# Decay attention with a low-rank mixer and feed-forward: ScalarE's casts of the next q and k set behind the newest exponential

## The chip, the cores and the metric

The kernel runs on 1 core of one Trainium2 chip, in one launch. The metric is device time in microseconds (us) of that core. Before the change it is 1206.89 us, the median of 3 runs (1206.88 to 1207.52).

## The reference

Eight batches of eight heads, 576 positions, 64 numbers per head. Attention with a learned decay comes first, then a block over the joined heads that mixes positions at low rank and applies a feed-forward layer. Cut to what is computed:

```python
scores = (q @ k.T) / 8                         # per batch and head, 576 x 576
cum    = cumsum(log(clip(f, 1e-4, 1)))
scores = where(causal, -1e9, scores + cum[:, None] - cum[None, :])
attn   = exp(scores - max(scores)); attn = attn / (sum(attn) + 1e-9)
x      = attn @ v                              # joined to 8 x 576 x 512
u      = x + ((x.T @ U @ V).T)                 # rank 32 over the positions
out    = u + relu(u @ w_ch1) @ w_ch2           # 512 -> 2048 -> 512
```

Everything is float32. The kernel gets that precision from a faster matmul format (fp32r) by splitting each operand into a high half, which is a cast, and a low half, which is the operand less its cast, and by adding two or three products.

## The kernel before, in words

**Two stages.** The first stage (to about 680 us) runs attention for all batches and the feed-forward for six of its sixteen column chunks, batch by batch. The second (from there to the end) runs the other ten chunks. The change is in the first.

**Steps and slots.** Heads are taken two at a time: 32 pairs, numbered 0 to 31. `step(t)` works on three pairs at once: scores of pair p, the turning of the probabilities of pair p-1 (called a) and their product with v, and the low-rank product of pair p-2 (called c). It has ten slots, s = 0 to 9. A slot first runs what earlier slots deferred to it (`run_later`, in order of a phase number), then issues its own TensorE work, and last some mixing or feed-forward units of an earlier batch. After every fourth pair come the mixing units of a whole batch; these steps are called mixing steps below.

**Names.** In the rows below the pair's number is left out. `S_10` is the score of half 1 (the second head) and row block 0; `St` are the two tails; `nm` the negated row maximum; `P_10` the exponential of `S_10`; `T_10` the transposed probabilities of half 1, group 0; `PTh` and `PTl` their high and low halves; `Tt` the low-rank product (U against x); `V` the product with v, and `cr` the copy of its lower rows. `G` are two operand tiles that hold the split q and k: G[0] for the first head (the first half) and G[1] for the second.

**One slot's chain.** For the score of one row block: TensorE forms it in one of two PSUM banks of the pool `psS` (lines 365 and 366), VectorE adds the mask and takes the row maximum (line 386), and ScalarE takes the exponential (line 394). The next score but one needs the bank, so TensorE waits for that exponential. Likewise a transposed group (line 461) lies in one of two banks of `psT`: ScalarE copies the high half (line 440), VectorE subtracts for the low half (line 443), and then the bank is free. In slot 8 the order on TensorE is S_12, T_12, Tt: Tt (line 630) takes the bank that T_11 of slot 7 had.

**The split of the next pair.** `parts(p, j, engines)` makes G[j] for pair p: two casts on ScalarE (line 328, q and k, 128 x 576 each), and on GpSimd a cast (line 328 again) and two subtractions (lines 343 and 344). The first half of pair p+1 is called in slot 6 of step p, after the last use of G[0]; the second half in slot 0 of the pair's own step.

**Who sets the order.** TensorE and SyncE (which issues the DMAs) run in the order in which the code is written. ScalarE, VectorE and GpSimd are ordered when the kernel is built, by a list scheduler that takes the written order, the dependencies and its own estimate of when each operand is there. `behind(ins, kind)` adds an edge without a semaphore: `ins` is ordered after the newest instruction of that kind. In the kernel before, the casts of the first half are set behind the exponential of the tails (line 422, kind "tail"), and those of the second half are free. For pair 6, the first one that is split, `pin` keeps the written order.

Of the kernel before, what the change touches and what calls it, by code (L numbers as in the profile page):

```python
# [36 lines left out]
NF = 6  # L37
# [3 lines left out]
def tile_decay_attention_moe(ctx, tc, qk, v, f, U, V, w1, w2, out):  # L41
    nc = tc.nc
# [8 lines left out]
    newest = {}  # L51

    def behind(ins, kind):
        tc.add_manual_dep(
            ins.ins, newest[kind].ins.name,
            mybir.DependencyInfo(mybir.DependencyClass.NoSync, mybir.DependencyReason.DATA), reason=f"order behind {kind}",
        )
# [104 lines left out]
    def decay_split(fr, dq, cm):  # L162
        nc.vector.tensor_scalar(cm[:, 2], fr, -8.0, None, op0=ALU.mult)
        nc.gpsimd.tensor_tensor(cm[:, 3], dq[:, 1], cm.bitcast(F32)[:, 2], op=ALU.subtract)
# [101 lines left out]
    def defer(phase, fn, slots=1):  # L266
        later.setdefault(now[0] + slots, []).append((phase, fn))

    def run_later():
        now[0] += 1  # L270
        for _, fn in sorted(later.pop(now[0], []), key=lambda x: x[0]):
            fn()
# [54 lines left out]
    def copy(eng, dst, src):  # L327
        return eng.copy(dst, src) if eng is nc.scalar else eng.tensor_copy(dst, src)  # L328

    def parts(p, j, engines):  # L330


        g, cols, own, oth = G[j], COLS[j], OWN[j], OTH[j]
        q, k = st[p]["qk"][j]
        gf = g.bitcast(F32)
        eq, ek, ek2, el, em = engines
        pin = tc.keep_in_program_order if p == NF else lambda x: x
        for eng, dst, src in ((eq, g[:, 0, cols], q), (ek, g[:, 2, cols], k)):
            cast = pin(copy(eng, dst, src))
            if j == 0 and p > NF:  # L340
                behind(cast, "tail")
        pin(copy(ek2, g[own, 3, cols], k[own]))
        pin(el.tensor_tensor(g[oth, 2, cols], k[oth], gf[oth, 2, cols], op=ALU.subtract))  # L343
        pin(em.tensor_tensor(g[own, 1, cols], q[own], gf[own, 0, cols], op=ALU.subtract))  # L344
# [13 lines left out]
    def qk_mm(ps, p, c0, cols, first, last, j):  # L358

        if p < NF:  # L360
            q, k = st[p]["qk"][j]
            nc.tensor.matmul(ps, q[:, c0 : c0 + P], k[:, cols], start=first, stop=last)  # L362
            return
        cols = slice(AOFF[j] + cols.start, AOFF[j] + cols.stop)
        nc.tensor.matmul(ps, G[j][:, 0, c0 : c0 + P], G[j][:, 2, cols], start=first, stop=False)  # L365
        nc.tensor.matmul(ps, G[j][:, 1, c0 : c0 + P], G[j][:, 3, cols], start=False, stop=last)  # L366
# [3 lines left out]
    def bank_s(p, name):  # L370

        scored[0] += 1
        if p < NF and scored[0] % 2:
            return psF.tile([P, 512], F32, tag="F", name=name)
        return psS.tile([P, 512], F32, tag="S", name=name)

    def score(p, j, i):
        z = st[p]
        w = P * (i + 1)
        ps = bank_s(p, f"S{p}_{j}{i}")  # L380
        c0 = AMAIN[j] + P * i
        qk_mm(ps[:, :w], p, c0, slice(0, w), True, True, j)
        col = 2 * i + j

        def top():
            newest["top"] = nc.vector.tensor_tensor_reduce(  # L386
                ps[:, :w], ps[:, :w], mask[:, 512 - w : 512], scale=-SCALE, scalar=3.0e38,
                op0=ALU.add, op1=ALU.min, accum_out=z["nm"][:, col : col + 1],
            )

        def use():
            pt = sb2.tile([P, w], F32, tag=f"P{i}", name=f"P{p}_{j}{i}")
            z["P"][j].append(pt)
            nc.scalar.activation(  # L394
                pt, ps[:, :w], AF.Exp, bias=z["nm"][:, col : col + 1], scale=-1.0, accum_out=z["sm"][:, col : col + 1]
            )

        defer(0, top)
        defer(2, use)
# [372 lines left out]
    NP = B * NHP  # L772
# [49 lines left out]
    def step(t):  # L822
        p = SEQ[t]
# [3 lines left out]
        nxt_p = p + 1 if ps_ else NP  # L827
# [6 lines left out]
        for s in range(6 + 2 if last else SLOTS):  # L834
            when = now[0] + 1

            def at(phase, fn):
                later.setdefault(when, []).append((phase, fn))

            if s == 0 and ps_ and p >= NF:  # L840
                at(5, lambda: parts(p, 1, ENGINES))
                place_decay(p, 1)
            if (t, s) == (1, 1):
                decay_split(fr, dq, cm0)
            if (t, s) == (2, 1):
                for j in range(2):
                    decay_negate(cm0, j)
                nc.vector.tensor_scalar(fl, cm0.bitcast(F32)[:, 2], 0.0, 1.0, op0=ALU.mult, op1=ALU.add)
            if (t, s) == (3, 2):
                decay_store(cm0, fl)  # L850
            if (t, s) == (NHP, 0):
                clear_operands()
            if s == 3 and pa and a >= NF:
                at(4, lambda: make_vs(a))
            if s == (9 if pa and a >= NF else 4) and pa:
                at(4, lambda: inverse(a))
            if s == 6 and NF <= nxt_p < NP:
                at(5, lambda: parts(p + 1, 0, ENGINES))
            if s == (4 if last else 5) and px:
                at(5, lambda: split_x(c))  # L860
            if (t, s) in DECODES:
                u = DECODES.index((t, s))

                steps = [lambda: load_w(u + (3 if u < 6 else 2)), lambda: decode_w(u)]
                if u < LATE:
                    for fn in steps if u < 8 else steps[::-1]:
                        at(6, fn)
                else:
                    at(6, lambda: decode_w(u, (0,)))
                    defer(6, lambda: decode_w(u, (1,)), 3)  # L870
                    defer(6, steps[0], 3)
            run_later()
            if s == 4 and ps_ and p > NF:
                load_v(p)
            if s == 1 and pa and 0 < a <= NF:
                load_v(a)
            if s == 0 and ps_ and p:
                load_qk(p + 1, 0)
            if s == 6 and ps_ and p:
                load_qk(p + 1, 1)  # L880
            if s == 7 and NF <= nxt_p < NP:
                place_decay(p + 1, 0)

            if ps_:
                if s < 4:
                    score(p, 0, s)
                elif s < 6:
                    score_tail(p, s - 4)
                elif s > 6:
                    score(p, 1, s - 6)  # L890
            if px and s == 0:
                values(c, 1)
            if pa and s < 3:
                turn_p(a, 0, s)
            if px and s == (2 if last else 3):
                turn_x(c)
            if s == (3 if last else 4) and (pa or px):
                turn_small(a if pa else None, c if px else None)
            if pa and s == 5:
                turn_tail(a)  # L900
            if pa and 6 <= s < 9:
                turn_p(a, 1, s - 6)
            if pa and s == 7:
                values(a, 0)
            if px and s == (6 if last else 8):
                ranks(c)

            if mixing:
                for _ in range(2 if t == MIX[0] and s < 3 else 1):
                    mixing.pop(0)[1]()  # L910
                for _ in range(1 if ending else (1, 1, 2, 1, 1)[s] if s < 5 else 0):
                    if filler:
                        run_filler()
            elif len(filler) > held(t) and s in ROOM:

                ahead = sum(x >= s for x in ROOM) + len(ROOM) * (min(m for m in MIX if m > t) - 1 - t)
                credit[0] += (len(filler) - held(t)) / max(ahead, 1)
                if credit[0] > 0.999 or t > LAST - 3:
                    credit[0] = max(credit[0] - 1, 0)
                    run_filler()  # L920
            if ps_ and s == 6:
                score(p, 1, 0)
            if last and s == 7:
                run_filler()
            if px and s == (6 + 1 if last else 9) and st[c]["hp"] == NHP - 1:
                b = st[c]["b"]
                assert len(filler) <= held(t) and not mixing
                mixing.extend(mix_units(b))
                nxt = ffn_units(b)
                pending.append(nxt)  # L930
            if not mixing and pending:
                assert not filler
                filler.extend(pending.pop())
# [715 lines left out]
```

## Time and profile before

| | before |
|---|---|
| median of 3 runs | 1206.89 us |
| time of the profiled execution | 1206.92 us |
| its span, first to last instruction | 1205.1 us |
| TensorE (PE) busy | 1183.8 us, 98% |
| VectorE (DVE) busy | 931.2 us, 77% |
| ScalarE (ACT) busy | 767.3 us, 64% |
| GpSimd (POOL) busy | 514.8 us, 43% |
| ScalarE casts into G (line 328) | 104, 65.4 us busy, 684 ns each |

The profiled execution takes 1.8 us more than its span and is within 0.03 us of the median. A row of the timeline gives the start in us, the duration in us, the engine, the line, the operation, what it writes and reads, the shape and how many were merged into the row; square brackets give the time for which the engine stood idle before it and what ended that. PEld is TensorE's loading of weights. A row of the waits gives who waited, for whom, the sum in us, how often, and the longest.

### The profile page before, as it was taken

Reading aid. Unit: us, or ns where it says so; the run is one execution under the profiler, and the core shown is the slowest. Engines: PE = TensorE matmul, PEld = TensorE weight load, DVE = VectorE, ACT = ScalarE, POOL = GpSimd, SP = SyncE. Lnnn points to the kernel's source line nnn. Section 1 sums busy time; section 2 is a strip of 40 time slices with the busy share of each in tenths; the row PEclk is TensorE's granted clock in tenths of the full one; section 3 lists DMA queues with packets and bytes.
Section 4 is the critical chain, followed back from the end, with each engine's and each line's share of the span. In section 5 each row is a group of like instructions: output and inputs, shape, how many; then the busy total and the mean of one; then the engine's idle time right before and its main releaser. Section 6 shows DMA issues by size and latency. Waiting matters only on the chain.

```text
span 1205.1 us, 23859 instructions
## 1 busy us (share of the span) xinstructions
PE 1183.8 (98%) x8460; PEld 1084.9 (90%) x8460; DVE 931.2 (77%) x2233; ACT 767.3 (64%) x2076; POOL 514.8 (43%) x506
## 2 busy tenths in 40 slices
PE   8999999999999999999999999999999999999998
PEld 5888898998998988989989997788999999999998
DVE  8987878778778678877686699976777867778675
ACT  8877786776868758767766577434454544545543
POOL 2215463553635435544442000024575555555553
PEclk9999999999999999999999999999999999999999
DMA  5754244335335325425322244533424344243420
GB/s 161 192 139 146 81 104 155 103 82 160 84 89 169 102 69 152 121 69 172 90 79 90 97 144 160 159 105 94 134 86 110 101 133 134 96 115 99 132 52 36
DMA packets 81159, 138.47 MB, mean 115 GB/s; under 512 B 8752, under 2 KB 45616, under 8 KB 78992
## 3 DMA queue, kind: packets, MB, share of 16 engines
q1 hardware_dynamic: 79824, 128.56, 35.4%
q0 software_dynamic: 1152, 8.39, 3.8%
q8 instruction: 67, 1.10, 0.4%
q14 instruction: 52, 0.43, 0.1%
q10 hardware_dynamic: 64, 0.00, 0.0%
HBM read 101.08 MB, written 35.78 MB: 114 GB/s over the span
## 4 chain that ended last, share of the span: by engine, by line
PE 83%; DVE 8%; ACT 6%; issue 1%; POOL 0%; ACTq 0%; DVEq 0%; POOLq 0%
PE N L1283 12%; PE A L723 12%; PE B L742 11%; PE A L1263 9%; PE B L1263 7%; PE V L564 5%; PE T L461 4%; PE S L365 3%; PE V L536 3%; PE S L366 2%; PE B L1283 2%; PE Tt L630 2%; PE S L362 2%; PE O L1348 1%; ACT G L328 1%
## 5 line engine op out<-in xcount | busy, mean ns | idle before, releaser
L394 ACT ACTIVATE P<-S,nm 128x128 f32<-128x128 f32 (+3 forms) x256 | 139.0, 545 | 54.5 <-DVE nm L386 48.8
L197 POOL TENSOR_TENSOR hb<-xn,hb 128x256 fp32r<-128x256 f32 x136 | 113.6, 856 | 125.5 <-ACT hb L194 108.0
L386 DVE CUSTOM_DVE_ANT_0 S<-S,mask 128x128 f32<-128x128 f32 (+3 forms) x256 | 125.8, 496 | 52.3 <-PE S L366 46.3
L328 POOL CAST G<-qk 64x576 fp32r<-64x576 f32 x52 | 35.4, 680 | 206.9 <-PE St L366 150.4
L723 PE MATMUL A<-uh,w1h 128*128 128x256 f32 (+1 forms) x384 | 119.7, 312 | 0.0
L723 PE MATMUL A<-ul,w1h 128*128 128x256 f32 (+1 forms) x384 | 113.6, 296 | 0.0
L723 PE MATMUL A<-uh,w1l 128*128 128x256 f32 (+1 forms) x384 | 113.5, 296 | 0.0
L194 ACT CAST hb<-xn 128x256 fp32r<-128x256 f32 x136 | 51.8, 404 | 77.3 <-DVE xn L1269 42.8
L443 DVE TENSOR_TENSOR PTl<-T,PTh 128x512 fp32r<-128x512 f32 (+1 forms) x156 | 79.0, 527 | 12.1 <-ACT PTh L440 11.1
L742 PE MATMUL B<-w2h,hh 128*128 128x512 f32 x216 | 88.2, 408 | 0.0
L461 PE MATMUL T<-ident,P 128*128 128x128 f32 x544 | 85.5, 273 | 0.0
L344 POOL TENSOR_TENSOR G<-qk,G 64x576 fp32r<-64x576 f32 x52 | 74.6, 1434 | 24.6 <-ACT G L328 24.3
L742 PE MATMUL B<-w2l,hh 128*128 128x512 f32 x216 | 85.0, 394 | 0.0
L742 PE MATMUL B<-w2h,hl 128*128 128x512 f32 x216 | 84.6, 392 | 0.0
L1283 PE MATMUL N<-sw,hb 128*128 128x256 f32 x546 | 80.4, 283 | 0.0
L1283 PE MATMUL N<-b2h,hb 128*128 128x256 f32 x420 | 79.9, 282 | 0.0
L343 POOL TENSOR_TENSOR G<-qk,G 64x576 fp32r<-64x576 f32 x52 | 75.0, 1442 | 10.9 <-issue 4.2
L365 PE MATMUL S<-G 128*128 128x128 f32 x208 | 70.8, 345 | 7.0 <-ACT P L394 5.8
L723 PEld LDWEIGHTS A<-uh,w1h 128*128 128x128 f32 x384 | 72.9, 190 | 0.9 <-DVE hl L728 0.2
L723 PEld LDWEIGHTS A<-uh,w1l 128*128 128x128 f32 x384 | 73.1, 190 | 0.5
L723 PEld LDWEIGHTS A<-ul,w1h 128*128 128x128 f32 x384 | 72.8, 190 | 0.0
L1283 PEld LDWEIGHTS N<-sw,hb 128*128 128x128 f32 x546 | 71.7, 190 | 0.4 <-POOL hb L197 0.2
(328 smaller groups left out, 4006.3 us busy)
## 6 DMA issues: line engine op xcount, KB each, us to landing
qk<-in_qk_dram SPq DMA_DIRECT2D x104, 288.0 KB
direct<-ud SPq DMA_DIRECT2D x48, 256.0 KB
sr<-in_w_dram SPq DMA_DIRECT2D x20, 512.0 KB
vr<-in_v_dram SPq DMA_DIRECT2D x32, 256.0 KB
accd<-ost SPq DMA_DIRECT2D x32, 256.0 KB
xn<-accd SPq DMA_DIRECT2D x8, 1024.0 KB
out_dram<-xn SPq DMA_DIRECT2D x32, 256.0 KB
ud<-uh SPq DMA_DIRECT2D x7, 1024.0 KB
```

The lines of the kernel that those rows point to most:

```text
L197: leng.tensor_tensor(dl, src, dh.bitcast(F32), op=ALU.subtract)
L343: pin(el.tensor_tensor(g[oth, 2, cols], k[oth], gf[oth, 2, cols], op=ALU.subtract))
L344: pin(em.tensor_tensor(g[own, 1, cols], q[own], gf[own, 0, cols], op=ALU.subtract))
L365: nc.tensor.matmul(ps, G[j][:, 0, c0 : c0 + P], G[j][:, 2, cols], start=first, stop=False)
L386: newest["top"] = nc.vector.tensor_tensor_reduce(ps[:, :w], ps[:, :w], mask[:, 512 - w : 512], scale=-SCALE, scalar=3.0e38, op0=ALU.add, o ...
L394: nc.scalar.activation(pt, ps[:, :w], AF.Exp, bias=z["nm"][:, col : col + 1], scale=-1.0, accum_out=z["sm"][:, col : col + 1])
L443: defer(2, lambda: nc.vector.tensor_tensor(dstl, src, dsth.bitcast(F32), op=ALU.subtract))
L461: nc.tensor.transpose(tp[:, P * x : P * x + P], z["P"][j][i][:, P * c : P * c + P], ident)
L723: nc.tensor.matmul(ps[:, :nt], wt[:, fc, c], ut[:, c, sl], start=m == 0, stop=m == 3 * NDC - 1)
L742: nc.tensor.matmul(ps, ht[:, fc, P * x : P * x + P], wt[:, fc], start=fc == 0 and m == 0, stop=fc == NA - 1 and m == 2,)
L1263: nc.tensor.matmul(ps, a[x][:, c], b[y][:, c], start=start and m == 0, stop=m == 5, skip_group_check=not start)
L1283: nc.tensor.matmul(ps[:, y], a[p_][:, P * y : P * y + P], w[q_], start=start and y == 0 and m == 0, stop=stop and y == 1 and m == 2,)
```

## The change

Two edits in `parts`, `score` and `step`:

- every exponential of a row block is noted as the newest of kind "exp", and for all pairs after 6 the ScalarE casts of both halves are set behind the newest one. In the first half this takes the place of the edge to the tail's exponential; in the second half there was none;
- the first half of the next pair is called in slot 7 instead of 6 (for pair 6 itself it stays in slot 6). GpSimd's cast and subtractions are called with it.

```diff
@@ parts @@
         for eng, dst, src in ((eq, g[:, 0, cols], q), (ek, g[:, 2, cols], k)):
             cast = pin(copy(eng, dst, src))
-            if j == 0 and p > NF:
-                behind(cast, "tail")
+            if p > NF:
+                behind(cast, "exp")
@@ score, use() @@
-            nc.scalar.activation(
+            newest["exp"] = nc.scalar.activation(
                 pt, ps[:, :w], AF.Exp, bias=z["nm"][:, col : col + 1], scale=-1.0, accum_out=z["sm"][:, col : col + 1]
             )
@@ step @@
-            if s == 6 and NF <= nxt_p < NP:
+            if s == (7 if nxt_p > NF else 6) and NF <= nxt_p < NP:
                 at(5, lambda: parts(p + 1, 0, ENGINES))
```

TensorE, SyncE and GpSimd keep their order of instructions. On ScalarE and VectorE the scheduler's order changes. Three places follow; a step without mixing units first.

ScalarE in slots 6 to 8 of pair 16's step (`qk_0` and `G_91` are the first half of pair 17), before:

```order
L422 ACTIVATE Ptl_4284,sm_4136<-St_1_4265,nm_4135 128x288
L328 CAST G_91<-qk_0_4147 128x576 x2
L440 CAST PTh_4166<-T_10_4297 128x512
L394 ACTIVATE P_10_4314,sm_4136<-S_10_4308,nm_4135 128x128
L440 CAST PTh_4166<-T_11_4320 128x384
L394 ACTIVATE P_11_4341,sm_4136<-S_11_4317,nm_4135 128x256
```

and with the change:

```order
L422 ACTIVATE Ptl_4284,sm_4136<-St_1_4265,nm_4135 128x288
L440 CAST PTh_4166<-T_10_4292 128x512
L394 ACTIVATE P_10_4309,sm_4136<-S_10_4303,nm_4135 128x128
L328 CAST G_91<-qk_0_4147 128x576 x2
L440 CAST PTh_4166<-T_11_4320 128x384
L394 ACTIVATE P_11_4341,sm_4136<-S_11_4317,nm_4135 128x256
```

The two casts went from in front of T_10's high half to behind P_10, and now stand in front of T_11's high half. So it is in 19 of the 24 steps of pairs 7 to 30 (the six mixing steps, of pairs 10, 14, 18, 22, 26 and 30, among them). In the other five (pairs 12, 15, 19, 20, 23) T_11's high half stands ahead of P_10 and so ahead of the casts.

VectorE in the same step, before:

```order
L386 ISA S_10_4308,nm_4135<-S_10_4308,mask 128x128
L386 ISA nm_4135 128x1
L386 ISA S_11_4317,nm_4135<-S_11_4317,mask 128x256
L386 ISA nm_4135 128x1
L443 TENSOR_TENSOR PTl_4167<-T_10_4297,PTh_4166 128x512
L443 TENSOR_TENSOR PTl_4167<-T_11_4320,PTh_4166 128x384
L386 ISA S_12_4345,nm_4135<-S_12_4345,mask 128x384
```

and with the change:

```order
L443 TENSOR_TENSOR PTl_4167<-T_10_4292,PTh_4166 128x512
L386 ISA S_10_4303,nm_4135<-S_10_4303,mask 128x128
L386 ISA nm_4135 128x1
L386 ISA S_11_4317,nm_4135<-S_11_4317,mask 128x256
L386 ISA nm_4135 128x1
L386 ISA S_12_4345,nm_4135<-S_12_4345,mask 128x384
L386 ISA nm_4135 128x1
L443 TENSOR_TENSOR PTl_4167<-T_11_4320,PTh_4166 128x384
```

T_10's low half went in front of S_10's row maximum, and T_11's low half behind that of S_12. In 18 of the 19 steps named above the low half of T_11 now stands behind S_12; the one in which it keeps its place in front is pair 7's. In the five others it keeps its place in front of S_12.

ScalarE in slots 8 to 0 around the second half's casts, in the mixing step of pair 26 (`qk_1` and `G_92` are the second half of pair 27, `Tu_3` and `Tv` mixing units), before:

```order
L667 CAST uh_6051<-Tu_3_7310 128x4x128
L328 CAST G_92<-qk_1_7233 128x576 x2
L667 CAST uh_6051<-Tv_7335 128x4x64
L394 ACTIVATE P_13_7345,sm_7037<-S_13_7332,nm_7036 128x512
L583 COPY cr_1_7360<-V_1_7359 64x576
L194 CAST VS_7449<-vr_7172 128x10x64
```

and with the change:

```order
L667 CAST uh_6051<-Tu_3_7310 128x4x128
L667 CAST uh_6051<-Tv_7335 128x4x64
L394 ACTIVATE P_13_7345,sm_7037<-S_13_7332,nm_7036 128x512
L328 CAST G_92<-qk_1_7228 128x576 x2
L583 COPY cr_1_7360<-V_1_7359 64x576
L194 CAST VS_7449<-vr_7172 128x10x64
```

The casts went from in front of P_13, the last exponential of the pair, to behind it, and now stand in front of the copy of V. It is so in every step of pairs 7 to 30; in some a relu of a feed-forward unit stands between.

## The prediction

> **What bounds the kernel now.** First the page, and then the waits of TensorE (PE, and PEld for its weight loads).
>
> ```profile
> span 1205.1 us, 23859 instructions
> PE 1183.8 (98%) x8460; PEld 1084.9 (90%) x8460; DVE 931.2 (77%) x2233; ACT 767.3 (64%) x2076; POOL 514.8 (43%) x506
> ...
> PEclk9999999999999999999999999999999999999999
> ...
> PE 83%; DVE 8%; ACT 6%; issue 1%; POOL 0%; ACTq 0%; DVEq 0%; POOLq 0%
> ...
> PE S L365 <- ACT P L394: 5.8, 14, 0.9
> PE Tv L686 <- DVE ul L668: 1.9, 6, 0.3
> PEld Tt L630 <- DVE PTl L443: 2.0, 8, 0.3
> ```
>
> PE is busy for all but 21 us of the span and carries 83% of the chain that ended last. So the span moves by what PE's idle time gains or loses, almost one to one. What the change can give back is small: 5.8 us in which a score waited for a bank that an exponential still held. The last row is a warning. In 8 steps the weight loads of Tt already wait for the low half L443 in the other pool of two banks, though no row of PE's own waits names Tt: there is no slack left at that place.
>
> **A step without mixing units.** Pair 16's step, from the timeline by engine:
>
> ```profile
> 322.23 1.26 ACT L328 CAST G<-qk 128x576 fp32r<-128x576 f32 x2
> 323.36 0.61 ACT L440 CAST PTh<-T 128x512 fp32r<-128x512 f32 x1
> 323.84 0.40 ACT L394 ACTIVATE P<-S,nm 128x128 f32<-128x128 f32 x1
> 324.19 0.51 ACT L440 CAST PTh<-T 128x384 fp32r<-128x384 f32 x1
> ...
> 323.35 0.30 DVE L386 CUSTOM_DVE_ANT_0 S<-S,mask 128x128 f32<-128x128 f32 x1 [0.53 <-PE S L366]
> 323.56 0.14 DVE L386 DVE_READ_ACCUMULATOR2_ANT nm<- 128x1 f32 x1
> 324.00 1.29 DVE L443 TENSOR_TENSOR PTl<-T,PTh 128x512 fp32r<-128x512 f32 x2
> 325.78 0.57 DVE L386 CUSTOM_DVE_ANT_0 S<-S,mask 128x384 f32<-128x384 f32 x1 [0.48 <-PE S L366]
> 326.26 0.75 DVE L584 TENSOR_TENSOR xT<-V,cr 64x576 f32<-64x576 f32 x1
> ...
> 325.40 0.34 PE L366 MATMUL S<-G 128*128 128x384 f32 x1
> 325.82 0.30 PE L630 MATMUL Tt<-xh,Us 128*64 128x128 f32 x1
> ```
>
> Here P_10 starts at 323.84, bound by its row maximum (323.56 + 0.14 = 323.70) rather than by the casts: the casts fill time in which ScalarE would wait. T_11's high half comes 0.35 behind it, both low halves are done at 325.29, and Tt starts at 325.82 in PE's own order.
>
> With the change ScalarE starts T_10's high half at 322.23 and ends it at 322.84. Its low half now goes before the row maximum of S_10 and takes about 0.65, to 323.5; the maximum then takes 0.35 (323.35 to 323.70 above) and P_10 starts at about 323.9. Nothing is gained there. Behind it stand the casts, 1.13 from the first cast's start to the next instruction (323.36 - 322.23). T_11's high half starts at 323.9 + 0.35 + 1.13 = 325.38 and ends at 325.89, 1.2 later than before. VectorE takes S_12 first: its scores end at 325.40 + 0.34 = 325.74, the maximum starts 0.04 later and leaves the engine after 0.48 (326.26 - 325.78). Then the low half of T_11 takes 0.56, and Tt starts 0.06 behind it. Both are seen in the mixing step of pair 26:
>
> ```profile
> 538.84 0.56 DVE L443 TENSOR_TENSOR PTl<-T,PTh 128x384 fp32r<-128x384 f32 x1
> ...
> 538.49 0.44 PE L365 MATMUL S<-G 128*128 128x384 f32 x1 [0.22 <-ACT P L394]
> 538.77 0.34 PE L366 MATMUL S<-G 128*128 128x384 f32 x1
> 539.46 0.28 PE L630 MATMUL Tt<-xh,Us 128*64 128x128 f32 x1
> 541.46 0.43 PE L686 MATMUL Tv<-ident,xn 64*128 64x64 f32 x4 [0.32 <-DVE ul L668]
> 544.72 0.39 PE L365 MATMUL S<-G 128*128 128x256 f32 x1 [0.50 <-ACT P L394]
> ...
> 542.46 1.25 ACT L328 CAST G<-qk 128x576 fp32r<-128x576 f32 x2
> 543.87 0.70 ACT L394 ACTIVATE P<-S,nm 128x512 f32<-128x512 f32 x1
> ```
>
> The low half ends at 539.40 and Tt follows at 539.46. So with the change Tt starts 0.04 + 0.48 + 0.56 + 0.06 = 1.14 behind the end of S_12's scores, say 1.13: at 326.87 in pair 16's step instead of 325.82. PE has nothing else to take meanwhile, since its order is fixed: a stall of **1.05 us**, where there was none. Twelve steps without mixing units have this order (pairs 8 to 29). The first and the last of them:
>
> ```profile
> 154.26 0.34 PE L366 MATMUL S<-G 128*128 128x384 f32 x1
> 154.69 0.30 PE L630 MATMUL Tt<-xh,Us 128*64 128x128 f32 x1
> ...
> 603.34 0.34 PE L366 MATMUL S<-G 128*128 128x384 f32 x1
> 603.91 0.28 PE L630 MATMUL Tt<-xh,Us 128*64 128x128 f32 x1
> ```
>
> They give 154.60 + 1.13 - 154.69 = 1.04 and 603.68 + 1.13 - 603.91 = 0.90. The ten between lie from 0.78 to 1.05 by the same two rows each, and the twelve add up to **+11.7**. In pair 7's step the low half keeps its place before S_12 and only the later high half counts, about **+0.6**. In the five steps where T_11's high half stays ahead of P_10, nothing is added at Tt.
>
> Does a later wait shrink in exchange? Not in these steps: PE idled nowhere else in them, and what follows (P_11, the copy of V, the second half's casts) comes later by no more than PE itself.
>
> **The six mixing steps.** Here ScalarE works without a break, so P_10 does come 1.15 earlier and the 0.22 before S_12 goes: its scores end at 538.27 + 0.62 = 538.89 and Tt at 540.02 instead of 539.46, later by 0.56. Then PE comes to Tv at 541.14 + 0.56 = 541.70, when the operand it idled 0.32 for is already there: 0.24 behind. At S_01 the second edit acts: P_13 starts at 543.87 - 1.15 = 542.72 and ends at 543.4, while PE arrives at 544.22 + 0.24 = 544.46 and no longer waits until 544.72. A mixing step gains 0.26; six of them **-1.6**.
>
> **The second half elsewhere.** It costs where nothing but the casts kept ScalarE busy before P_13 and the copy of V was ready. Pair 15's step:
>
> ```profile
> 309.64 1.24 ACT L328 CAST G<-qk 128x576 fp32r<-128x576 f32 x2
> 310.80 0.68 ACT L394 ACTIVATE P<-S,nm 128x512 f32<-128x512 f32 x1
> 311.59 0.64 ACT L583 COPY cr<-V 64x576 f32<-64x576 f32 x1
> 312.88 0.37 ACT L394 ACTIVATE P<-S,nm 128x128 f32<-128x128 f32 x1
> ...
> 310.55 0.08 DVE L386 DVE_READ_ACCUMULATOR2_ANT nm<- 128x1 f32 x1
> 313.70 0.34 PE L365 MATMUL S<-G 128*128 128x384 f32 x1
> ```
>
> The maximum is there at 310.63, so P_13 moves from 310.80 to 310.66 only; the casts (0.35 behind, 1.16 long) push the copy from 311.59 to 312.15, and the next pair's P_00 by as much, to end at 313.81. S_02 takes that bank 0.15 behind an exponential's end (543.87 + 0.70 to 544.72 above), at 313.96 instead of 313.70: 0.25. Three steps are so (pairs 8, 15, 23): **+0.8**. In the others the copy waits for its product, and the casts lie in that wait.
>
> One more score waited once, where G[1]'s casts stood before P_12:
>
> ```profile
> 116.58 0.30 PE L365 MATMUL S<-G 128*128 128x128 f32 x1 [0.66 <-ACT P L394]
> ```
>
> That goes, but work on ScalarE and VectorE that does not follow PE stands close behind it, so I take -0.3 between -0.66 and 0.
>
> **What is hidden.** GpSimd's subtractions of the first half start with the casts, up to 2.9 later. They still end before the next S_00, which comes 2.3 to 5.2 behind them now; in the tightest steps it is a tenth of a microsecond, which I leave out. The 25 + 26 pairs of casts are as many and as long as before, and no DMA moves.
>
> **Sum.** 11.7 + 0.6 - 1.6 + 0.8 - 0.3 = +11.2, onto the profiled execution's 1206.92 (its span and the 1.8 around it): **1218**. The median of the runs, 1206.89, is the same to 0.03.
>
> By the Trainium skill, "Perfetto Trace Analysis", section "Tensor Engine Instruction (MATMUL, LD_WEIGHTS)", VectorE and ScalarE take their instructions strictly in queue order. By that the low half waits behind S_12's maximum, and the sum is as above. The trace agrees as far as it goes, since its rows stand in the program's order on both engines. Without that rule the second rival's sum would hold.
>
> **Rivals.**
> - *The stall at Tt is covered.* PEld waits 0.3 there now without a loss of PE. If the modelled ends hide a cover of over 1.05 per step, only the gains are left: 6 x 0.50 at S_01 (the 0.22 is lost again at Tv, which waits for VectorE) and 0.66, so 1206.92 - 3.7 = 1203. Against it: Tt's rows already start 0.06 behind the low half, so there is no time left before them to hide it in.
> - *Only ScalarE's delay counts.* If the low half went as soon as its high half is there, Tt would come 2.63 behind P_10's start (0.35 + 1.13 + 0.51 + 0.64): 326.53 in pair 16's step, 0.71 late. By the same steps the thirteen give 6.5 and the mixing steps gain 0.5 each: 1206.9 + 6.5 - 3.0 + 0.5 = 1211. Against it: the order on VectorE is fixed in the program.
> - *More stalls behind the first.* The copy of V, the next pair's first exponentials or G[0] come late too in most steps. At the 0.25 of pair 15 in all 24 steps that adds 5: 1223. Against it: Tt's stall puts PE back by more than what follows is put back.
> - *No change*: gains and stalls cancel, which needs stalls of 0.2 per step; nothing in the rows gives that.
> - *The clock falls.* If the short stalls let the granted clock drop to half for one slot (a tenth of a 19 us step) in each of 19 steps, 19 x 1.9 = 36 are added: 1254. The row PEclk above, the granted clock in tenths, shows a 9 (90% or more) in every slice, with the idle times of the rows above in them. The Trainium skill ("TensorE: Matmul & The Clock Gate", section "A second HAM failure mode: psum-queue depth-cycling") tells of a kernel whose frequent short PE idles made the clock go back and forth; by that rule this rival would hold, and the trace of before does not show it.
>
> **Chances.** The forecast with its own range 1214 to 1221: 0.65. Only ScalarE's delay: 0.13. More stalls: 0.07. Covered: 0.09. No change: 0.05. The clock: 0.01. The range reaches down to the second rival and up to the third's lower part, 1209 to 1222; it leaves out the covered case, no change, the clock and some of the third. A change within 0.2% (2.4 us), about what a measurement of this kernel can tell from none, is "same": 0.06. Slower: 0.85. Faster: 0.09.
>
> **What would show it.** Right: PE's waits name Tt waiting for PTl (L443), some 18 times and 13 to 17 us; the waits of S for P fall from 5.8 to about 3; S_01's 0.50 and S_12's 0.22 in the mixing steps are gone; PE's busy time and the second stage stay. Wrong: no PE row for Tt, or the maximum of S_12 starting after the low half of T_11, or a new wait of S for POOL's G.

## The result, and the profile after

| | before | after |
|---|---|---|
| median | 1206.89 us (4 runs, 1206.62 to 1207.52) | 1221.62 us (4 runs, 1221.54 to 1222.07) |
| profiled execution, span | 1206.92, 1205.1 us | 1221.60, 1219.8 us |
| TensorE busy | 1183.8 us | 1184.8 us |

The ratio is 1.0123, with a 95% interval from 1.011 to 1.0136: the change makes the kernel 14.7 us slower, where 11.2 were forecast. The 1221.62 us lie 0.6 above the forecast's own range (1214 to 1221) and inside the whole range (1209 to 1222), in the part of it that reached up to the rival of more stalls. First the page of the changed kernel and its waits of PE and PEld (who waited, for whom, us in all, times, longest):

```profile
span 1219.8 us, 23881 instructions
PE 1184.8 (97%) x8460; PEld 1084.9 (89%) x8460; DVE 924.4 (76%) x2233; ACT 768.4 (63%) x2076; POOL 514.3 (42%) x506
...
PE Tt L630 <- DVE PTl L443: 18.4, 19, 1.0
PE S L365 <- ACT P L394: 2.9, 5, 0.9
...
PEld S L365 <- POOL G L343: 0.6, 2, 0.3
```

A wait that PE did not have before heads the list: Tt for the low half of T_11, 19 times: 1.00 in 18 steps and 0.40 in pair 7's. The waits of scores for exponentials fell from 5.8 to 2.9, and PE's work is the same to 1 us, at a granted clock of 1.00 in both stages, as before. The step of pair 16, whose rows of before stand in the prediction, now reads so on ACT, DVE and PE:

```profile
329.29 0.37 ACT L394 ACTIVATE P<-S,nm 128x128 f32<-128x128 f32 x1 [1.02 <-DVE nm L386]
329.65 1.23 ACT L328 CAST G<-qk 128x576 fp32r<-128x576 f32 x2
330.78 0.48 ACT L440 CAST PTh<-T 128x384 fp32r<-128x384 f32 x1
...
331.34 0.57 DVE L386 CUSTOM_DVE_ANT_0 S<-S,mask 128x384 f32<-128x384 f32 x1 [1.71 <-ACT PTh L440]
...
331.82 0.55 DVE L443 TENSOR_TENSOR PTl<-T,PTh 128x384 fp32r<-128x384 f32 x1
...
330.68 0.34 PE L365 MATMUL S<-G 128*128 128x384 f32 x1
330.86 0.34 PE L366 MATMUL S<-G 128*128 128x384 f32 x1
...
332.52 0.24 PE L630 MATMUL Tt<-xh,Us 128*64 128x128 f32 x1 [1.00 <-DVE PTl L443]
333.09 0.45 PE L365 MATMUL S<-G 128*128 128x512 f32 x1
```

The chain is the one that was forecast, in its order: the scores of S_12 end at 331.20, its maximum starts at 331.34, the low half of T_11 at 331.82, Tt at 332.52. VectorE stood idle for 1.71 us ahead of the maximum, and the casts now stand right in front of T_11's high half. The row names that high half, which ends at 331.26, as what ended VectorE's wait; it is a coincidence of this step, since the maximum starts as far behind the scores in all the steps of pairs 8 to 30, also in the mixing steps, where the high half ends 0.04 behind the maximum's start. ScalarE waits 1.02 for P_10's row maximum, time in which the casts ran before.

Two numbers of a stall must be kept apart. The row says 1.00 idle. From the start of S_12 to the start of S_13 (both line 365) it took 326.45 - 325.22 = 1.23 before and takes 333.09 - 330.68 = 2.41 now, which is 1.18 more:

```profile
325.22 0.34 PE L365 MATMUL S<-G 128*128 128x384 f32 x1
...
326.45 0.44 PE L365 MATMUL S<-G 128*128 128x512 f32 x1
```

Matmuls overlap in the rows (each starts ahead of the modelled end of the one before), and idle time counts from an end. So the idle time is too small by 0.2 here, and losses below are taken from start to start, of the same matmuls in two traces.

### The profile page after: what moved, and what is told of

Read it like the earlier page. It is cut to its first block, busy times and chain, and to the rows that moved or that the text cites. A ratio compares the mean times of both kernels' runs of the same rounds, so it can differ in the third digit from the quotient of the medians.

```text
span 1219.8 us, 23881 instructions
## 1 busy us (share of the span) xinstructions
PE 1184.8 (97%) x8460; PEld 1084.9 (89%) x8460; DVE 924.4 (76%) x2233; ACT 768.4 (63%) x2076; POOL 514.3 (42%) x506
## 4 chain that ended last, share of the span: by engine, by line
PE 78%; DVE 9%; ACT 9%; issue 2%; DMA 1%; SPq 0%; POOL 0%; DVEq 0%; ACTq 0%; POOLq 0%
PE N L1283 12%; PE B L742 10%; PE A L723 10%; PE A L1263 9%; PE B L1263 7%; PE V L564 4%; PE T L461 3%; PE V L536 3%; PE S L365 2%; PE B L1283 2%; PE S L366 2%; ACT P L394 2%; PE S L362 2%; PE O L1348 1%; ACT PTh L440 1%
```

## The experiments

Eight kernels, each a small edit of the kernel before or of the changed one. Times are medians; e1 to e4 ran on one chip and e5 to e8 on another, with the kernel before beside them each time (1206.6 to 1207.0).

| | edit | us | ratio to before, 95% |
|---|---|---|---|
| e1 | first half of the change alone | 1222.98 | 1.0135, 1.012 to 1.015 |
| e2 | second half alone | 1209.17 | 1.0019, 1.001 to 1.0028 |
| e3 | the change, T_11's low half ahead of S_12's maximum | 1214.74 | 1.0067, 1.005 to 1.0084 |
| e5 | the change, casts behind T_11's high half | 1211.90 | 1.0041, 1.0027 to 1.0054 |
| e4 | before, both halves moved at mixing steps, and pair 7's second half | 1205.65 | 0.9987, 0.9978 to 0.9997 |
| e6 | before, second half behind P_00 after mixing steps | 1202.97 | 0.9965, 0.9952 to 0.9979 |
| e7 | e6, and the copy of V behind a mixing unit's cast | 1201.85 | 0.9957, 0.9945 to 0.997 |
| e8 | as e6, after all steps | 1206.14 | 0.9994, 0.9984 to 1.0004 |

**e1 and e2: which half loses.** e1 leaves the second half's casts free, e2 leaves the first half's as they were.

```diff
 # e1, against the change
-            if p > NF:
+            if j == 0 and p > NF:
                 behind(cast, "exp")
 # e2, against the change
-                behind(cast, "exp")
+                behind(cast, "exp" if j else "tail")
...
-            if s == (7 if nxt_p > NF else 6) and NF <= nxt_p < NP:
+            if s == 6 and NF <= nxt_p < NP:
```

> The change's first half alone (slot 7, behind the newest exponential); the second half's casts free as in the kernel before. My theory, that the loss stands at Tt: 18 stalls of 1.0 us idle in front of Tt stay, each 1.19 from start to start, the waits of S for P in the mixing steps and in pair 7 come back, the waits of S_02 behind pairs 8, 15 and 23 go. Sum 13.3 (twelve steps) + 0.6 (pair 7) + 0 (mixing steps) = 1220.5 to 1221. Rival, that the second half's edge carries a good part of the loss: 1210 to 1216.

> The change's second half alone; the first half's casts in slot 6 behind the tail's exponential as before. My theory: no stall at Tt; S_01 gains 0.75 in six mixing steps and S_02 loses 0.39, net -2.2; S_02 loses 2.8 in three steps (pairs 8, 15, 23); pair 7 gains 0.7. Sum about 0: 1206 to 1207.5. Rival, that the second half carries a good part of the loss: 1210 or more.

PE's waits of e1:

```profile
PE Tt L630 <- DVE PTl L443: 19.0, 19, 1.0
PE S L365 <- ACT P L394: 4.1, 8, 0.9
```

and of e2:

```profile
PE S L365 <- ACT P L394: 5.5, 16, 0.9
...
PE Tt L630 <- DVE PTl L443: 1.7, 1, 1.7
```

The stalls at Tt belong to the first half; the rival falls. Both kernels are about 2 us over their expectation. In e1 the step of pair 7, where the decoding of weights shares VectorE, is 2.3 longer than before and not 0.6: there is a new wait of 0.9 at S_03, and 1.0 at Tt instead of 0.4, since the low half of T_11 stands behind S_12's maximum in this step too. Its S_00 still comes 0.8 earlier, which was not expected, and the steps of pairs 16 and 24 are 0.4 to 0.5 longer each than their stall. In e2 pair 7's step is 1.6 longer (1.7 at Tt). The ten runs of e2 spread from 1207.6 to 1211.2, four of them under 1208; the trace is of one at 1209.55, and whether every run has the 1.7 is not shown. In e2 the rest goes as expected: the six mixing steps gain 0.24 each, and S_02 loses 0.83 each behind pairs 8, 15 and 23. Two mixing steps (pairs 10 and 18) lose another 0.4 to 0.5, which I had not expected; its cause is open. The halves do not add up: 16.4 and 2.6 against 14.7 together. By the starts 2.3 of the 4.3 over lie at pair 7, where each half alone makes a wait that the change does not have (at S_03 in e1, the 1.7 at Tt in e2); the rest is in small pieces.

**e3: order on VectorE, or lateness on ScalarE.** One edge, without a semaphore, puts T_11's low half back ahead of S_12's maximum. ScalarE keeps the order of the change.

```diff
-        defer(0, top)
+        defer(0, lambda: (top(), (j, i) == (1, 2) and p > NF and behind(newest["top"], "low")))
...
-        defer(2, lambda: nc.vector.tensor_tensor(dstl, src, dsth.bitcast(F32), op=ALU.subtract))
+        defer(2, lambda: newest.update(low=nc.vector.tensor_tensor(dstl, src, dsth.bitcast(F32), op=ALU.subtract)))
```

> The whole change, with T_11's low half ordered ahead of the row maximum of S_12 on VectorE (one edge without a semaphore); ScalarE's order is that of the change, row for row. My theory, that Tt waits for the maximum and the low half one after the other: the idle time at Tt falls from 1.00 to 0.3 to 0.55, since T_11's high half ends 0.03 before to 0.18 behind the scores of S_12 and the low half takes 0.55: 1211 to 1213. Rival, that ScalarE's delay alone makes the stall: no change, 1221.6. A second rival, that the maximum put back by the low half delays P_12 and the scores that need its bank: 1215 to 1219.

PE's waits of e3, and pair 16's step on DVE and PE:

```profile
PE Tt L630 <- DVE PTl L443: 7.4, 19, 0.5
...
PE Tv L686 <- DVE ul L668: 1.9, 6, 0.3
...
329.36 0.56 DVE L443 TENSOR_TENSOR PTl<-T,PTh 128x384 fp32r<-128x384 f32 x1 [1.66 <-ACT PTh L440]
329.84 0.56 DVE L386 CUSTOM_DVE_ANT_0 S<-S,mask 128x384 f32<-128x384 f32 x1
...
329.98 0.28 PE L630 MATMUL Tt<-xh,Us 128*64 128x128 f32 x1 [0.41 <-DVE PTl L443]
```

The idle time at Tt falls as expected, from 1.00 to between 0.3 and 0.5, and the kernel gains 6.9 us. So lateness on ScalarE makes less than half of the stall by itself: in the twelve steps 5.8 of the 13.3 us are left with the order put right, and 7.5 go with the maximum that stood in front of the low half. The order without the lateness was not run. By the rows it would be enough for the whole stall, since in all 18 steps of the change the high half had ended 0.4 or more before the maximum left VectorE and the low half could start. The expectation was 2 us too low, because it also counted a gain in the six mixing steps. There the wait of Tv, which the change had covered, is back (1.9), and the step is as long as before, or longer by 0.1 to 0.5 in three of the six (not followed up).

**e5: the place of the casts.** In the steps without mixing units the casts go one place further, behind T_11's high half.

```diff
             if p > NF:
-                behind(cast, "exp")
+                behind(cast, "exp" if j or p % NHP == NHP - 1 else "high")
...
-        defer(0, lambda: nc.scalar.copy(dsth, src))
+        defer(0, lambda: newest.update(high=nc.scalar.copy(dsth, src)))
...
-            if s == (7 if nxt_p > NF else 6) and NF <= nxt_p < NP:
+            if s == ((7 if nxt_p % NHP == NHP - 1 else 8) if nxt_p > NF else 6) and NF <= nxt_p < NP:
```

> The whole change, but in the steps without mixing units the first half's casts are called in slot 8 and set behind T_11's high half, one place later on ScalarE than in the change (P_10, T_11's high half, casts); VectorE then has T_11's low half ahead of S_12's maximum. Mixing steps and pair 7's first half as in the change. My theory, that it is the place of the casts between P_10 and T_11's high half, not their lateness: no idle at Tt in the twelve steps (-13.3 against the change's 1221.6), S_13 perhaps 0.1 to 0.3 late in them, since P_11 now stands behind the casts: 1209 to 1212. Rival, that casts that come late cost it wherever they stand (P_11 and S_13, or GpSimd's subtractions and the next S_00): 1215 to 1222.

PE's waits of e5, and its ScalarE in pair 16's step:

```profile
PE S L365 <- ACT P L394: 6.6, 15, 0.9
PE Tt L630 <- DVE PTl L443: 6.0, 6, 1.0
...
326.21 0.47 ACT L440 CAST PTh<-T 128x384 fp32r<-128x384 f32 x1
326.57 1.26 ACT L328 CAST G<-qk 128x576 fp32r<-128x576 f32 x2
327.72 0.48 ACT L394 ACTIVATE P<-S,nm 128x256 f32<-128x256 f32 x1
```

Only the six mixing steps still wait at Tt. In the twelve others the casts run later than in the change and nothing is lost at Tt or S_13: T_11's high half must not stand behind them, and P_11 can. Lateness of the casts is not the cause of the stall at Tt. Most of what e5 loses on top lies in the five steps where T_11's high half stood ahead of P_10 (pairs 12, 15, 19, 20, 23): there the casts now precede P_10, and all five scores S_12 wait 0.6 for it, which is 4.1 in all from start to start. Another 1.4 goes in the steps of pairs 9, 17 and 25. In the last two VectorE is held up by GpSimd: in pair 17's step its instruction of line 435 takes 1.35 instead of 0.17 and ends 0.03 behind GpSimd's subtraction (the last section tells of this); that it makes their whole loss is not shown:

```profile
332.04 1.35 DVE L435 TENSOR_SCALAR sm<-sm 128x9 f32<-128x9 f32 x1
...
331.93 1.43 POOL L344 TENSOR_TENSOR G<-qk,G 64x576 fp32r<-64x576 f32 x1 [1.05 <-ACT G L328]
```

**e4: the mixing steps.** The kernel before, with the casts moved at the mixing steps: the first half's behind T_11's high half, the second half's behind the newest exponential and the newest cast of a turned mixing unit. Two more edges are in it: pair 7's second half behind the newest exponential, and S_13's maximum in the mixing steps behind the newest low half of a mixing unit.

```diff
-            if j == 0 and p > NF:
-                behind(cast, "tail")
+            if p > NF and (j == 0 or p == NF + 1 or p % NHP == NHP - 1):
+                j and p > NF + 1 and p % NHP == NHP - 1 and behind(cast, "uh")
+                behind(cast, "exp" if j else "high" if p > NF + 1 and p % NHP == NHP - 1 else "tail")
...
-        defer(0, top)
+        defer(0, lambda: (top(), (j, i) == (1, 3) and p > NF and p % NHP == NHP - 2 and behind(newest["top"], "ul")))
...
-            if s == 6 and NF <= nxt_p < NP:
+            if s == (8 if nxt_p > NF + 1 and nxt_p % NHP == NHP - 1 else 6) and NF <= nxt_p < NP:
```

> The kernel before, with the casts moved only around the six mixing steps: there the first half's are called in slot 8 and set behind T_11's high half (so behind P_10 and it), the second half's behind the newest exponential and the newest cast of a turned mixing unit, and the maximum of S_13 behind the newest low half of a mixing unit; pair 7's second half behind the newest exponential. My theory: in a mixing step the waits at S_12 (0.47 from start to start), Tv (0.36) and S_01 (0.75, of which 0.39 goes back at S_02) shrink without a stall at Tt, but GpSimd's subtractions of the first half, 1.1 ahead of the next S_00 in the change, come 0.5 later and the scores 0.8 earlier: a wait of 0.3 there. Six times 0.6 to 1.2 and 0.7 of pair 7: 1199 to 1203. Rival, that these waits only move to the next place that ScalarE serves: 1206 to 1208.

PE's waits, and pair 26's step on ACT, DVE and PE:

```profile
PE Tv L686 <- DVE ul L668: 5.7, 6, 0.9
...
538.70 0.64 ACT L583 COPY cr<-V 64x576 f32<-64x576 f32 x1
539.36 0.59 ACT L667 CAST uh<-Tu 128x512 fp32r<-128x512 f32 x1
...
540.04 0.67 DVE L668 TENSOR_TENSOR ul<-Tu,uh 128x512 fp32r<-128x512 f32 x1
...
540.86 0.24 PE L686 MATMUL Tv<-ident,xn 64*128 64x64 f32 x1 [0.94 <-DVE ul L668]
```

The time, 1205.65, lies between the theory and the rival. The rival holds for the first half. S_12's wait is gone and Tt does not wait, but Tv now idles 0.94 instead of 0.32; from start to start the mixing step is unchanged to 0.00. ScalarE works there without a break up to the cast of the third turned unit (line 667, at 539.36), and Tv waits for what follows from it. Whatever is exchanged in front of that cast only moves PE's wait. This is also why the change could stall 1.00 at Tt in each mixing step and lose only 0.1 by Tv. Pair 7's edge (1.7 at Tt again) costs e4 0.4 instead of gaining 0.7.

**e6 and e7: what can be gained.** At S_01 the wait was real. In e6 the second half's casts after a mixing step go behind P_00; they stand before P_13 in the kernel before and right behind it in the change. Nothing else moves on ScalarE; on VectorE the scheduler shifts some instructions of these steps, and on GpSimd the subtraction for VS (line 197) goes ahead of those for G[1]. e7 also puts the copy of V behind the cast at which Tv's chain ends, and the scheduler then takes that unit's low half earlier on VectorE.

```diff
-            if j == 0 and p > NF:
-                behind(cast, "tail")
+            if p > NF and (j == 0 or p > NF + 1 and p % NHP == NHP - 1):
+                behind(cast, "exp" if j else "tail")
...
-                at(5, lambda: parts(p, 1, ENGINES))
+                defer(5, lambda: parts(p, 1, ENGINES), 2 if p > NF + 1 and p % NHP == NHP - 1 else 1)
 # e7 besides
-        defer(1, lambda: nc.scalar.copy(cr, pv[D:P, X0 : X0 + S]))
+        defer(*((3.5, lambda: behind(nc.scalar.copy(cr, pv[D:P, X0 : X0 + S]), "uh")) if (j, p % NHP) == (0, 1) and p > NF else (1, lambda: nc.scalar.copy(cr, pv[D:P, X0 : X0 + S]))))
...
-            defer(3, lambda: nc.scalar.copy(dh, src))
+            defer(3, lambda: newest.update(uh=nc.scalar.copy(dh, src)))
```

> The kernel before with one move: in the steps that follow the six mixing steps (pairs 11, 15, 19, 23, 27, 31) the second half's casts are called in slot 1 and set behind the newest exponential, which puts them behind P_00. First halves, and all other second halves, as before. My theory: P_13 comes 1.15 earlier, so S_01 gains its 0.75, and P_00 no longer stands behind the casts, so S_02 does not give 0.39 back; GpSimd has 4.2 of slack for G[1] in the change, of which this uses 2: six times 0.75, 1202 to 1202.7. Rival, that ScalarE is the bound there and hands the wait to the next score: 1204.5 to 1206.

> As the kernel with casts behind P_00 after the mixing steps, and in the mixing steps the copy of V's lower rows (first half) behind the cast of the third turned mixing unit, which ends 0.64 earlier on ScalarE. My theory, that in a mixing step Tv is where TensorE meets ScalarE's chain: Tv's 0.32 goes (0.36 from start to start), 2 us in all: 1199.8 to 1200.8. Rival, that the chain has another end just behind it (P_12 or P_13 and the scores that need their banks): no gain against the other, 1202 to 1203.

PE's waits of e6:

```profile
PE S L365 <- ACT P L394: 2.8, 8, 0.9
PE Tv L686 <- DVE ul L668: 1.9, 6, 0.3
```

and of e7, with one row of its timeline:

```profile
PE S L365 <- ACT P L394: 3.8, 14, 0.9
...
538.33 0.30 PE L365 MATMUL S<-G 128*128 128x128 f32 x1 [0.17 <-ACT P L394]
```

e6 gains 0.66 in each of six steps, 4.0 us in all, 0.3 short of the theory's range: S_01 comes 0.75 earlier and gives 0.1 back at the tails. e7 takes Tv's wait away, but two thirds of it return at the next S_00 (0.17 idle, six times), which waits for P_12; 1.1 us are left, between the theory and its rival. e7 is the fastest kernel of this study, 0.43% faster than the kernel before.

**e8: the same move everywhere.** As e6, without the condition on mixing steps.

```diff
-            if j == 0 and p > NF:
-                behind(cast, "tail")
+            if p > NF and (j == 0 or p > NF + 1):
+                behind(cast, "exp" if j else "tail")
...
-                at(5, lambda: parts(p, 1, ENGINES))
+                defer(5, lambda: parts(p, 1, ENGINES), 2 if p > NF + 1 else 1)
```

> The kernel before with the second half's casts of all pairs after 7 called in slot 1 and set behind the newest exponential, so behind P_00; first halves as before. Against the kernel with the second half's edge of the change alone, the casts move from in front of the copy of V and P_00 to behind both. My theory, that the three waits of S_02 (pairs 8, 15, 23, 2.5 together) come from the copy and P_00 standing behind 1.16 of casts: they go, and so do the 0.39 of S_02 behind the mixing steps; the time is that of the same move at the mixing steps alone, 1202.3 to 1203.5. Rival, that casts behind the newest exponential cost in the steps without mixing units wherever they stand (T_00's high half and the product with it, or GpSimd's subtractions before the tails): 1205 to 1209.

The time, 1206.14, lies in the rival's range, and its interval does not tell it from the kernel before. In the mechanism each side was half right. Against e2 the three waits of S_02 and the 0.4 behind the mixing steps are gone, so these come from the copy and P_00 behind the casts, as the theory said. But behind P_00 the casts stand in front of T_00's high half and P_01, and in nine steps without mixing units S_03 and the tails come later, by 0.15 to 0.7, together 3.3: the gain of e6 is spent. By the starts of the matmuls the nine are pairs 8, 9, 12, 16, 17, 20, 24, 25 and 28.

## Why the prediction was right, and where not

By its own steps, from start to start:

| step of the prediction | forecast | measured |
|---|---|---|
| Tt in twelve steps without mixing units | +11.7 | +13.3 |
| Tt in pair 7's step | +0.6 | +0.6 |
| six mixing steps | -1.6 | -1.4 |
| the second half elsewhere (S_02 behind pairs 8, 15, 23) | +0.8 | +2.8 |
| pair 7's S_00 | -0.3 | -0.7 |
| not forecast (pair 12's step -0.3, and smaller) | 0 | -0.1 |
| after the attention | 0 | +0.2 |
| sum | +11.2 | +14.7 |

**The mechanism held.** Tt waits for the low half, which waits for S_12's maximum, which waits for PE's own scores; the idle time is 1.00 in all of the 18 steps, however far ScalarE is behind. The second rival (ScalarE's delay alone) falls: it needs the low half to go as soon as its high half is there, and in the change the maximum went first. What it priced, 6.5 in thirteen steps, is what e3 measured with that order put right (5.8, and 0.6 in pair 7's). By the Trainium skill, "Perfetto Trace Analysis", section "Tensor Engine Instruction (MATMUL, LD_WEIGHTS)", ScalarE and VectorE take their queues strictly in order; e3 agrees, since one exchange on VectorE took 6.9 us away. The falling clock did not come either: PE's busy time is the same to 1 us and the granted clock is 1.00. The tenth of a microsecond that was left out for GpSimd's subtractions is there, as 0.1 from start to start behind pairs 15 and 23 (the PEld row of S for POOL's G above). The "25 + 26 pairs of casts" are 26 + 26 (104 casts in the table of before); no term hangs on it.

**First mis-sized term: each stall (1.6 of the 3.5 us by which the sum was too low).** The step "Tt starts 0.04 + 0.48 + 0.56 + 0.06 = 1.14 behind the end of S_12's scores" came out at 332.52 - 331.20 = 1.32. The maximum starts 0.14 behind the scores, not 0.04, and Tt 0.15 behind the low half, not 0.06. Both follow from the same thing, told in the last section.

**Second mis-sized term: S_02 (2.0 of them).** The step "the casts (0.35 behind, 1.16 long) push the copy" took 0.35 from an exponential of 128 columns, while P_13 has 512. Pair 15's step after the change:

```profile
315.28 0.69 ACT L394 ACTIVATE P<-S,nm 128x512 f32<-128x512 f32 x1 [0.65 <-DVE nm L386]
315.96 1.23 ACT L328 CAST G<-qk 128x576 fp32r<-128x576 f32 x2
317.22 0.64 ACT L583 COPY cr<-V 64x576 f32<-64x576 f32 x1
318.51 0.37 ACT L394 ACTIVATE P<-S,nm 128x128 f32<-128x128 f32 x1
...
319.02 0.44 PE L365 MATMUL S<-G 128*128 128x384 f32 x1 [0.63 <-ACT P L394]
```

The casts start 315.96 - 315.28 = 0.68 behind P_13 and the copy 1.26 behind them: 0.43 more than I took. P_13 itself is 0.2 later than forecast against PE (PE is 4.43 later than before at this place, so 310.66 became 310.85). Together 0.25 + 0.43 + 0.2 = 0.88, and 0.85 to 1.0 were measured from start to start, three times (0.63 idle in the row), with GpSimd's 0.1 in the two larger ones. The rival "more stalls behind the first" was nearest to this, with 0.25 in 24 steps; it is 0.9 in three, and e1 and e8 show it to be the second half's alone.

**The mixing steps: a right sum from a wrong split.** P_10 came earlier and S_12's wait went, as said. Tt then took 0.93 and Tv gave 0.36 back, in all +0.10 to the end of the step. S_01 gained 0.75, but S_02 lost 0.39 of it, since there too the copy and P_00 stand behind the casts. I had neither the second loss nor the true size of the gain, and that the sum came out so near my -0.26 a step is chance. In pair 26's step of the change Tt idles, and Tv and S_01 no longer do:

```profile
551.72 0.24 PE L630 MATMUL Tt<-xh,Us 128*64 128x128 f32 x1 [1.00 <-DVE PTl L443]
...
553.31 0.46 PE L686 MATMUL Tv<-ident,xn 64*128 64x64 f32 x4
...
555.84 0.36 PE L365 MATMUL S<-G 128*128 128x256 f32 x1
```

e4 shows what was missed: the step has a bound of its own on ScalarE, up to Tv.

## What to carry to other kernels

An instruction may be moved only past work that no one waits for in that stretch: these casts cost nothing at Tt behind a high half and 0.8 to 1.2 us a step in front of it. Before moving work on an engine that is not the bottleneck, list which bank each of its instructions frees, who takes that bank next, and what now stands between them on both engines. In a stretch where that engine works without a break, only what stands behind its last awaited instruction can be moved with gain, as e6 did and e4 did not.

## What the runs showed of the hardware that was not expected

**An instruction that waits for two engines starts 0.1 us later.** The maximum of S_12 starts 0.04 behind its scores in pair 16 before the change, and 0.15 in pair 13 of the same trace (scores to 262.15):

```profile
261.81 0.34 PE L366 MATMUL S<-G 128*128 128x384 f32 x1
...
262.30 0.57 DVE L386 CUSTOM_DVE_ANT_0 S<-S,mask 128x384 f32<-128x384 f32 x1 [0.63 <-PE S L366]
```

The two instructions as built, with the engines whose semaphores they wait for (pair 16's, then pair 13's, and pair 16's after the change):

```
L386 ISA S_12_4345,nm_4135<-S_12_4345,mask 128x384 [waits PE_49]
L386 ISA S_12_3476,nm_3232<-S_12_3476,mask 128x384 [waits PE_49,Activation_49]
L386 ISA S_12_4345,nm_4135<-S_12_4345,mask 128x384 [waits PE_49,Activation_49]
```

In the trace before, all 11 maxima of S_12 that wait for PE alone, and find VectorE free, start 0.04 behind the scores (unrounded times), and the 4 that also wait for ScalarE 0.15. After the change 23 wait for both and all start 0.15 behind. When the low half stood in front, its own wait for ScalarE had done the second one's work; put behind, it left that wait to the maximum. The wait for ScalarE was long over in these cases: having two is what costs, not the second one's lateness. In the trace one of the two waits is an instruction of its own, which the timeline leaves out. These rows count them, with their shortest, median and longest duration in ns (line 386 before and after the change, where 5 and then 23 of them belong to S_12; and line 630 after it, where before there is none):

```profile
L386 DVEq EVENT_SEMAPHORE  x16: 21/21/21, 102.0 to 625.1; - x16
L386 DVEq EVENT_SEMAPHORE  x34: 21/21/21, 102.0 to 643.1; - x34
L630 PEldq EVENT_SEMAPHORE  x18: 51/51/51, 155.7 to 644.2; - x18
```

In pair 16's step after the change this instruction starts 0.04 behind the scores, where the maximum itself started before, and the maximum 0.11 behind it. Tt waits for VectorE and PE in the 18 steps that stall and starts 0.15 behind its operand in all of them; in pair 26's step before the change it waits for VectorE alone and starts 0.06 behind.

**Some of VectorE's instructions whose operands are all in SBUF are held up while GpSimd subtracts.** Pair 7's step in e2, DVE and POOL:

```profile
131.39 1.27 DVE L434 TENSOR_TENSOR sm<-sm 128x1 f32<-128x1 f32 x1
132.92 1.75 DVE L76 TENSOR_TENSOR w2l<-stg,w2h 128x512 fp32r<-128x512 f32 x1
...
131.20 1.44 POOL L344 TENSOR_TENSOR G<-qk,G 64x576 fp32r<-64x576 f32 x1 [0.57 <-ACT G L328]
132.71 1.41 POOL L343 TENSOR_TENSOR G<-qk,G 64x576 fp32r<-64x576 f32 x1
```

and the same two instructions before the change:

```profile
131.21 0.68 DVE L76 TENSOR_TENSOR w2l<-stg,w2h 128x512 fp32r<-128x512 f32 x1
132.61 0.15 DVE L434 TENSOR_TENSOR sm<-sm 128x1 f32<-128x1 f32 x1
```

In e2 both end just behind GpSimd's subtractions (at 132.66, the first subtraction at 132.64; and at 134.67, the second at 134.12 and most of the 0.68 that L76 takes alone behind it). The 1.7 at Tt in pair 7 is the low half that stands behind them. The kernel before has it too: of the instructions of line 435 (128x9, alone 0.17), 18 start while GpSimd subtracts; they take 0.26 to 0.44, and each ends 0.03 behind the subtraction. Not every instruction in SBUF is held: reciprocals of 128x9 and copies of 64x1 keep their 0.22 and 0.15. VectorE's instructions that read PSUM in the same stretch keep their times. The Trainium skill states such a sharing ("GPSIMD Engine Reference", section "8. Key points": the engine shares its SBUF interfaces with VectorE, whose instructions contend for them with two SBUF inputs or in a 2-port perf mode); the rows of lines 434 and 76, which have two, agree. I had looked only at the order on GpSimd and at what waits for it, not at whom it slows meanwhile.
